# S4 convolution and gated MLP, forward and backward: one PSUM bank for two gradient turns, one product for two planes, other spacing of the lonely transforms

## The chip, the cores and the metric

The kernel runs on one core of a Trainium2 chip, in one launch. The metric is the device time of an execution in microseconds. The chip's engines are called PE (TensorE, matmuls; its weight loads are PEld), DVE (VectorE), ACT (ScalarE), POOL (GpSimd) and SP (SyncE, which here only issues DMAs). Each engine executes its own instructions in the order in which they stand in its queue, and waits there for semaphores of the others.

## What is computed

The forward pass and the gradients (a vjp with `grad_out`) of a layer that adds an S4 convolution and a gated MLP to its input. Shapes: L = 2048 tokens, D = 576 channels, N = 128 states, F = 4608 hidden columns, all bfloat16.

```python
xn = _layernorm(x)
# A: S4. K[d,l] = Re sum_n C[d,n] exp(dt[d] A[d,n] l) dt[d] B[d,n], a causal convolution
Kf = rfft(pad(K)); Uf = rfft(pad(xn.T))
y  = irfft(Uf * Kf)[:, :L].T + xn * Dskip
# B: gated MLP
gate = xn @ W_gate; up = xn @ W_up
gate = gate * (gate > 0)
h = gate * up
out = x + y + h @ W_down
# returned: out, and the gradients for x, A, B, C (re and im), log_dt, Dskip, W_gate, W_up, W_down
```

## The kernel before

Two streams of work are woven into one program. The MLP stream (class `Ffn`, called FFN here) keeps TensorE busy from end to end; the S4 stream (class `S4`) is put between its matmuls.

**FFN.** F is cut into 12 chunks of 384 columns (the loop over `c`), each into 3 blocks `ft` of 128. The tokens are 4 groups `sg` of 4 x 128. For one `(c, sg, ft)`, `a_unit` makes three products of 5 matmuls with 512 columns: gate and up from `xT`, and dh from `gT` (L244). Relu, masks and products on ACT and DVE (L253 to L261) turn them into a tile `T` with three planes: h, and the gradients of gate and up. The planes are needed in two orientations. `outdx` uses them as they are (L298, with the weights `wf`) and gives the outputs `osx`, which POOL's queue adds up in DRAM as `acc_dram` (L311). The weight gradients `dw_down` (L336), `dw_gu` (L352) and `dw_left` (L370) need them turned, in `hN`, `dgN` and `duN`: that is the work of `t_steps` (L270), four transposes of 128x128 into a PSUM tile `ps_mm` and a copy out of it for each plane. The steps of `t_steps` are handed out by `a_unit`, one round after each of its three products, for units that were computed earlier (`turns`), and by `outdx` after its products. `ps_mm` has 5 PSUM banks, the S4 stream's `ps_s4` has 3. Each chunk loads the weights `wd0` to `wd2` through SP's queue (L187) and `wf`, 1296 KB, through ACT's (L191).

**S4.** The channels are two parts `hf` of 288. The convolutions are Fourier transforms in three stages that go through DRAM between them. A forward transform (`fwd1`, L625, then `mix`, L642) makes 16 first steps `n2`, stored as `A_...` (L629), and then 16 mixings `h` that each load a piece of all of these (L706, L774). `product` multiplies spectra on DVE (L664 to L671), `unmix` (L652) and `back2` (L683) go back. `p1` transforms the input and the gradient and brings back `dk`, the gradient of the convolution kernel: `bC1` tiles are loaded (L735) from `C_dk`, which the unmixing stores (L727). `params` computes the coefficient planes `pw` and 36 steps `ex_step` of exponentials: DVE, ACT, and a store of the tile `exs` to `ex_dram` (L585 to L587), with 8 buffers. `p2` generates the convolution kernel and its gradients, 16 channels at a time: DVE makes `xa` (L841), sine and cosine, A, B, X and `XC` (to L866), `turn` makes the kernel's columns (L904), stores them to `k_dram` (L907), transposes and copies `YT`, and `sums` reduces (L928 to L933). `p3` transforms the kernel, loaded as `kk` (L762), and makes the outputs' spectra, stored to `C_ydu` (L793).

`S4.gen` runs: constants; `both(p1(0), params)`; `both(p2(0), p1(1))`; `both(p2(1), p3(0))`; `p3(1)`. `both` weaves a second generator into the first in the ratio of two stated weights. So `p1(0)` and `p3(1)`, with no kernel generation beside them, are the lonely transforms; they have deeper buffers (n = 4 instead of 2).

**What sets the order.** Every generator yields a stated cost in us. The main loop takes FFN's steps one after the other and draws S4's steps as long as S4's stated sum is below `PACE` = 0.9 times FFN's. A larger stated cost in an S4 stage spreads it over more FFN work; `slow(f, task)` multiplies the stated costs of a task by f, and `gap` is a stated cost between stages, in which loads are to land. From the program that is written down in this way, a scheduler orders each engine's queue. `Balance` sends a PSUM copy (L62 on DVE, L68 on ACT) to the engine with the smaller stated sum. The last chunk's `outdx` adds S4's results for each 128 tokens and completes outputs (class `Final`); all of S4 must stand ahead of it.

Memory is reused: the tiles of `p2` (`xa`, `W`) lie where `params` had its buffers.

Of the kernel before, what the change touches and what calls it, by code (L numbers as in the profile page):

```python
# [9 lines left out]
BF16 = mybir.dt.bfloat16  # L10
F32 = mybir.dt.float32
# [12 lines left out]
NK = 5  # L24
# [136 lines left out]
class Ffn:  # L161
    def __init__(self, g, ctx, Wd_in, Wf_in, dWg, dWu, dWd):
        self.g = g
        self.Wd_in, self.Wf_in, self.dWg, self.dWu, self.dWd = Wd_in, Wf_in, dWg, dWu, dWd
        tc, nc = g.tc, g.nc
        pool = lambda name, bufs: ctx.enter_context(tc.tile_pool(name=name, bufs=bufs))
        wp = pool("ffn_w", 1)
        self.wd = [wp.tile([P, NK, Fc], BF16, name=f"wd{i}") for i in range(3)]
        self.wf = wp.tile([P, 3, FTC, D], BF16, name="wf")
        self.hN = wp.tile([P, ST, Fc], BF16, name="hN")  # L170
        self.dgN = wp.tile([P, ST, Fc], BF16, name="dgN")
        self.duN = wp.tile([P, ST, Fc], BF16, name="duN")
# [57 lines left out]
    def a_unit(self, c, sg, ft, turns=()):  # L230

        g, nc = self.g, self.g.nc
        src = self.t_steps(turns)
        xT, gT = self.X[(c, sg)]
        fs = slice(ft * P, (ft + 1) * P)
        pss = []
        dhb = self.dh0.get(ft) if (c, sg) == (0, 0) else None
        for i, rhs in enumerate((xT, xT, gT)):
            if i == 2 and dhb is not None:
                continue  # L240
            w = self.wd[i]
            ps = g.psum_mm.tile([P, 512], F32, name="ps_mm")
            for k in range(NK):
                nc.tensor.matmul(ps[:], lhsT=w[:, k, fs], rhs=rhs[:, k, :], start=(k == 0), stop=(k == NK - 1))  # L244
            pss.append(ps)
            for _ in turns:
                next(src)
            yield NK * 0.2158 + len(turns) * 0.22
        ps_g, ps_u = pss[0:2]
        shp = [P, JS * P]  # L250
        ru = self.ep.tile([P, 2, JS * P], BF16, name="rg")
        upm, rg = ru[:, 0], ru[:, 1]
        nc.scalar.activation(rg, ps_g[:], ACT.Relu)  # L253
        nc.vector.scalar_tensor_tensor(upm, rg, 0.0, ps_u[:], op0=ALU.is_gt, op1=ALU.mult)  # L254
        T = self.tp.tile([P, 3, JS * P], BF16, name="T")
        nc.vector.tensor_tensor(T[:, 0], rg, upm, op=ALU.mult)  # L256
        g.bal.add(d=1.6, a=0.48)
        if dhb is None:
            dhb = self.ep.tile(shp, BF16, name="dhb")[:]
            g.bal.copy(dhb, pss[2][:], 512)  # L260
        nc.vector.tensor_tensor(T[:, 1:3], dhb.unsqueeze(1).to_broadcast([P, 2, JS * P]), ru[:], op=ALU.mult)  # L261
        self.T[(c, sg, ft)] = tuple(T[:, i] for i in range(3))

    def t_steps(self, units):
        g, nc = self.g, self.g.nc
        for c, sg, ft in units:
            for src, dst in zip(self.T[(c, sg, ft)], (self.hN, self.dgN, self.duN)):
                pt = g.psum_mm.tile([P, 512], F32, name="ps_mm")[:].bitcast(BF16).rearrange("p (k t) -> p k t", t=P)
                for j in range(JS):
                    nc.tensor.transpose(out=pt[:, j, :], in_=src[:, j * P:(j + 1) * P], identity=g.ident_bf[:])  # L270
                g.bal.copy(dst[:, sg * JS:(sg + 1) * JS, ft * P:(ft + 1) * P], pt[:, 0:JS, :], 512, fp32=False)
                yield

    def outdx(self, c, sg, j, last=None, turns=()):
# [201 lines left out]
class S4:  # L476
# [85 lines left out]
    def params(self, pw):  # L562
# [3 lines left out]
        with ExitStack() as c:  # L566
            pool = self.pool(c, "par_raw", 1)
            exp_ = self.pool(c, "par_ex", 8)
            raw = pool.tile([P, 6, D], BF16, name="raw")
            nc.sync.dma_start(raw[:], self.par_in[:])  # L570
            ldt = pool.tile([P, D], BF16, name="ldt")
            nc.sync.dma_start(ldt[:], self.log_dt.rearrange("(o d) -> o d", o=1).to_broadcast([P, D]))
            yield 1.0
            dt = pool.tile([P, D], F32, name="dtf")
            nc.scalar.activation(dt[:], ldt[:], ACT.Exp)
            nc.sync.dma_start(self.dt_dram[:], dt[:])
            Ar, Ai, Br, Bi, Cr, Ci = (raw[:, i, :] for i in range(6))
            v.tensor_tensor(pw[:, 0, :], Ar, dt[:], op=ALU.mult)
            bal.add(d=0.7, a=0.7)
            yield 1.0  # L580

            def ex_step(i):
                shp = [P, SX, NE]
                ex = exp_.tile(shp, F32, name="exs")
                v.tensor_tensor(ex[:], pw[:, 0, i * SX:(i + 1) * SX].unsqueeze(2).to_broadcast(shp), self.ev[:].unsqueeze(1).to_broadcast(shp), op=ALU.mult)  # L585
                nc.scalar.activation(ex[:], ex[:], ACT.Exp)
                nc.sync.dma_start(self.ex_dram[:, i], ex[:])  # L587
                bal.add(d=0.75, a=0.65)

            p1 = pool.tile([P, D], F32, name="p1")  # L590
            p2 = pool.tile([P, D], F32, name="p2")
            v.scalar_tensor_tensor(pw[:, 1, :], Ai, 1.0 / TWO_PI, dt[:], op0=ALU.mult, op1=ALU.mult)
            for j, (y1, y2, op) in enumerate(((Br, Bi, ALU.subtract), (Bi, Br, ALU.add))):
                v.tensor_tensor(p1[:], Cr, y1, op=ALU.mult)
                v.tensor_tensor(p2[:], Ci, y2, op=ALU.mult)
                v.tensor_tensor(p1[:], p1[:], p2[:], op=op)
                v.tensor_tensor(pw[:, 2 + j, :], p1[:], dt[:], op=ALU.mult)
                bal.add(d=2.6)
                yield 2.0
            for i in range(D // SX):  # L600
                ex_step(i)
                yield 1.0

# [82 lines left out]
    def p1(self, hf, n, gap):  # L686
# [3 lines left out]
        with ExitStack() as c:  # L690
            ap = self.pool(c, f"p1_a{hf}", n, "right")

            def load(m):
# [1 line left out]
                nc.sync.dma_start(t[:, 0], g.xn_dram[:, 2 * m:2 * m + 2, cols])  # L695
                nc.sync.dma_start(t[:, 1], g.g_v[:, 2 * m:2 * m + 2, cols])
                return lambda i, n2: t[:, i, n2 % 2, :]
            yield from self.slow(1.0 if n < 4 else 1.8, self.fwd1(hf, 2, load, ap, self.pool(c, f"p1_o{hf}", 2 * n - 2 * (n < 4), "right"), n, gap))
        with ExitStack() as c:
            bp = self.pool(c, f"p1_b{hf}", n, "right")  # L700
            fp = self.pool(c, f"p1_f{hf}", n, "right")
# [5 lines left out]
                return b  # L707
            bs = Ahead(load_b, ST, n)
            Z = None
            f = 1.0 if n < 4 else 1.1  # L710
            for h in range(ST + 1):
                old, Z = Z, None
                if h < ST:
# [15 lines left out]
        with ExitStack() as c:  # L729
# [8 lines left out]
            for n2 in range(ST):  # L738
# [7 lines left out]
                g.bal.copy(dk[:, :, n2 % 4, :], self.back2(S3[:, n2 % 2], Ct, 0).rearrange("p (g d) -> p g d", d=SC), DH)  # L746
                if n2 % 4 == 3:
                    nc.sync.dma_start(self.dk_dram[hf][:, n2 // 4], dk[:])
                yield 0.5 if n < 4 else 1

    def p3(self, hf, n, gap):

        g, nc, bal = self.g, self.g.nc, self.g.bal
        with ExitStack() as c:
# [4 lines left out]
            def load(m):  # L759
# [46 lines left out]
    def p2(self, hf, pools, pw):  # L806
# [17 lines left out]
        for gi in range(DH // SC):  # L824
# [7 lines left out]
            for x0 in range(0, SC, SX):  # L832
# [28 lines left out]
                xw = [P, SX, 32]  # L861
                w1 = xp.tile(xs, F32, name="xa")[:].rearrange("p d e -> p (d e)")[:, 0:SX * 32].rearrange("p (d e) -> p d e", e=32)
                w2 = xp.tile([P, 2, SX, NE], F32, name="W")[:].rearrange("p r d e -> p (r d e)")[:, 0:SX * 32].rearrange("p (d e) -> p d e", e=32)
# [72 lines left out]
    def param_grads(self, hf, Sm, pw, xp, yop):  # L936
# [13 lines left out]
        pA, pB, cr, ci = (pw[:, i, hs] for i in range(4))  # L950
# [64 lines left out]
    def gen(self):  # L1015
# [4 lines left out]
        with ExitStack() as cp:  # L1020
# [231 lines left out]
```

## Time and profile before

| What | Value |
|---|---|
| Runs | 1819.53 us median of 3 (1813.02 to 1819.76) |
| Profiled execution | 1819.53 us; span of its instructions 1817.8 us |
| Mean granted clock of PE | 0.987 |
| DMA | 373.30 MB in 239003 packets, mean 205 GB/s |
| Transposes of the turns, L270 on PE | 1728, busy 158.0 us; idle before them 6.2 us |
| Copies of the turns on ACT, 128x512 bf16 | hN 138 x 593 ns, dgN 141 x 600 ns, duN 135 x 606 ns |
| Copies of YT on ACT, 128x1024 bf16 | 1012 ns in most |
| The two coefficient products on DVE, 128x512 f32 | L864 36 x 684 ns, L865 36 x 683 ns |
| wf loads | 11 through ACT's queue, 1296 KB each, median 9.3 us to landing |

A share of busy time is an average over very different stages, so the text below goes by stretches of time, and within a stretch by what an engine waited for. An idle engine costs nothing as long as PE has work; a wait of DVE or ACT counts where a matmul needs the PSUM bank that a copy behind it would free. Matmuls overlap in the pipeline: five with 512 columns in a row start 1.08 us before the work after them, though one is shown with 0.38 us.

### The profile page before, as it was taken

Reading aid. Unit: us, or ns where it says so; the run is one execution under the profiler, and the core shown is the slowest. Engines: PE = TensorE matmul, PEld = TensorE weight load, DVE = VectorE, ACT = ScalarE, POOL = GpSimd, SP = SyncE. Lnnn points to the kernel's source line nnn. Section 1 sums busy time; section 2 is a strip of 40 time slices with the busy share of each in tenths; the row PEclk is TensorE's granted clock in tenths of the full one; section 3 lists DMA queues with packets and bytes.
Section 4 is the critical chain, followed back from the end, with each engine's and each line's share of the span. In section 5 each row is a group of like instructions: output and inputs, shape, how many; then the busy total and the mean of one; then the engine's idle time right before and its main releaser. Section 6 shows DMA issues by size and latency. Waiting matters only on the chain. (4 is left out here: it accounts for less than half of the span.)

```text
span 1817.8 us, 42080 instructions
## 1 busy us (share of the span) xinstructions
PE 1726.3 (95%) x16449; PEld 1188.6 (65%) x16449; DVE 1321.4 (73%) x2875; ACT 1186.7 (65%) x2728; POOL 203.7 (11%) x246
## 2 busy tenths in 40 slices
PE   7979987999999999999999999999999999999998
PEld 5655546667666766767766756666676675576776
DVE  7565875476888878778687789889988864775551
ACT  5865863588488578568558658747756755664651
POOL 0200101021011011111101101201111100110000
PEclk9989988999999999999999999999999999999999
DMA  8789979678667666866856856766675578895873
GB/s 292 266 307 307 325 203 290 183 163 224 195 159 190 206 176 127 245 183 152 232 148 174 238 157 135 195 189 161 148 219 141 102 209 244 240 303 177 262 250 99
DMA packets 239003, 373.30 MB, mean 205 GB/s; under 512 B 49490, under 2 KB 153428, under 8 KB 237268
## 3 DMA queue, kind: packets, MB, share of 16 engines
q1 hardware_dynamic: 212836, 304.09, 51.9%
q0 software_dynamic: 24384, 51.92, 18.6%
q10 hardware_dynamic: 1584, 14.60, 2.2%
q8 instruction: 129, 2.11, 0.5%
q14 instruction: 70, 0.57, 0.1%
HBM read 233.10 MB, written 137.43 MB: 204 GB/s over the span
## 5 line engine op out<-in xcount | busy, mean ns | idle before, releaser
L298 PE MATMUL ps_mm<-wf,T 128*128 128x288 bf16 x3456 | 481.3, 287 | 9.1 <-DVE T L256 5.6
L298 PEld LDWEIGHTS <-T 128*128 128x128 bf16 x3456 | 323.0, 98 | 94.9 <-issue 9.6
L68 ACT CAST osx<-ps_mm 128x288 bf16<-128x288 f32 x684 | 260.8, 426 | 51.7 <-PE ps_mm L298 49.4
L311 POOL DMA_DIRECT2D acc_dram<-osx x160 | 138.2, 864 | 1057.1 <-ACT osx L68 543.2
L352 PEld LDWEIGHTS <-rows 128*128 128x128 bf16 x1536 | 146.3, 98 | 95.9 <-issue 4.6
L244 PE MATMUL ps_mm<-xT,wd_150 128*128 128x512 bf16 x720 | 182.9, 382 | 4.1 <-ACT xT L153 1.6
L270 PEld LDWEIGHTS <-T 128*128 128x128 bf16 x1728 | 128.0, 99 | 87.4 <-issue 7.4
L244 PE MATMUL ps_mm<-xT,wd_151 128*128 128x512 bf16 x720 | 180.2, 380 | 0.0
L244 PE MATMUL ps_mm<-gT,wd_152 128*128 128x512 bf16 x705 | 179.0, 384 | 1.0 <-ACT dgN L68 0.6
L270 PE MATMUL ps_mm<-ident_bf,T 128*128 128x128 bf16 x1728 | 158.0, 221 | 6.2 <-DVE rg L254 1.9
L336 PE MATMUL ps_mm<-rows,hN 128*128 128x144 bf16 x2304 | 158.4, 228 | 0.0
L336 PEld LDWEIGHTS <-hN 128*128 128x128 bf16 x2304 | 150.1, 99 | 3.7 <-issue 1.0
L254 DVE SCALAR_TENSOR_TENSOR rg<-rg,ps_mm 128x512 bf16<-128x512 bf16 x144 | 98.4, 683 | 68.0 <-PE ps_mm L244 41.1
L68 ACT CAST obw<-ps_mm 128x384 bf16<-128x384 f32 x103 | 49.1, 477 | 139.6 <-PE ps_mm L352 98.1
L352 PE MATMUL ps_mm<-dgN,rows 128*128 128x384 bf16 x768 | 137.3, 326 | 0.0
L352 PE MATMUL ps_mm<-duN,rows 128*128 128x384 bf16 x768 | 136.8, 326 | 0.0
L68 ACT CAST dhb<-ps_mm 128x512 bf16<-128x512 f32 x141 | 84.1, 596 | 60.0 <-PE ps_mm L244 58.5
L253 ACT ACTIVATE rg<-ps_mm 128x512 bf16<-128x512 f32 x144 | 87.3, 606 | 49.1 <-PE ps_mm L244 47.0
L261 DVE TENSOR_TENSOR T<-dhb,rg 128x1024 bf16<-128x1024 bf16 x141 | 98.9, 701 | 26.7 <-ACT dhb L68 26.0
L244 PEld LDWEIGHTS <-wd_150 128*128 128x128 bf16 x720 | 67.1, 98 | 65.4 <-issue 7.6
L244 PEld LDWEIGHTS <-wd_152 128*128 128x128 bf16 x705 | 64.0, 98 | 61.0 <-issue 4.4
L244 PEld LDWEIGHTS <-wd_151 128*128 128x128 bf16 x720 | 64.8, 98 | 59.4 <-issue 2.3
(2506 smaller groups left out, 3048.3 us busy)
## 6 DMA issues: line engine op xcount, KB each, us to landing
acc_dram<-osx POOLq DMA_DIRECT2D x176, 288.0 KB, 5.2
gT<-in_gT_dram SPq DMA_DIRECT2D x48, 640.0 KB, 6.1
xT<-xT_dram SPq DMA_DIRECT2D x44, 640.0 KB, 5.7
rows<-in_gq_dram SPq DMA_DIRECT2D x48, 576.0 KB, 4.7
wf<-in_Wf_dram ACTq DMA_DIRECT2D x11, 1296.0 KB, 9.3
ex_dram<-exs SPq DMA_DIRECT2D x36, 320.0 KB, 4.2
ex<-ex_dram SPq DMA_DIRECT2D x36, 320.0 KB, 4.7
out_dram<-obw SPq DMA_DIRECT2D x96, 96.0 KB, 2.7
```

What stands on the lines that cost most here:

```text
L68: self.nc.scalar.copy(out, in_)
L244: nc.tensor.matmul(ps[:], lhsT=w[:, k, fs], rhs=rhs[:, k, :], start=(k == 0), stop=(k == NK - 1))
L253: nc.scalar.activation(rg, ps_g[:], ACT.Relu)
L254: nc.vector.scalar_tensor_tensor(upm, rg, 0.0, ps_u[:], op0=ALU.is_gt, op1=ALU.mult)
L261: nc.vector.tensor_tensor(T[:, 1:3], dhb.unsqueeze(1).to_broadcast([P, 2, JS * P]), ru[:], op=ALU.mult)
L270: nc.tensor.transpose(out=pt[:, j, :], in_=src[:, j * P:(j + 1) * P], identity=g.ident_bf[:])
L298: nc.tensor.matmul(ps[:, cs], lhsT=lt, rhs=rh, start=(i == 0), stop=(i == len(mms) - 1))
L311: nc.gpsimd.dma_start(g.acc_dram[:, t, :, :], o[:], accum_op=ALU.add)
L336: nc.tensor.matmul(ps[:, ft * 144:(ft + 1) * 144], lhsT=self.hN[:, st, ft * P:(ft + 1) * P], rhs=gq[:, st, :], start=(st == 0), stop=(st = ...
L352: nc.tensor.matmul(ps[:, :Fc], lhsT=xs[:, st, 0:P], rhs=src[:, st, :], start=(st == 0), stop=(st == ST - 1))
```

## The change

Three things.

**Turns.** `dgN` and `duN` become two halves of one tile `gN`. `t_steps` now has two steps a unit: the four transposes of h with a copy of 512 columns, then the eight transposes of both gradients into one PSUM tile with one copy of 1024. `a_unit` hands them out in thirds: for one unit in `turns` none after the gate product, one after up, one after dh; for two units 1, 1 and 2. The stated cost of all turns of a unit is the same (0.66).

```diff
-            for _ in turns:
+            n = (2 * len(turns) * (i + 1)) // 3 - (2 * len(turns) * i) // 3
+            for _ in range(n):
                 next(src)
-            yield NK * 0.2158 + len(turns) * 0.22
+            yield NK * 0.2158 + n * 0.33
...
-            for src, dst in zip(self.T[(c, sg, ft)], (self.hN, self.dgN, self.duN)):
+            src, js, fs = self.T[(c, sg, ft)], slice(sg * JS, (sg + 1) * JS), slice(ft * P, (ft + 1) * P)
+            for which in ((0,), (1, 2)):
+                n = len(which) * JS
                 pt = g.psum_mm.tile([P, 512], F32, name="ps_mm")[:].bitcast(BF16).rearrange("p (k t) -> p k t", t=P)
-                for j in range(JS):
-                    nc.tensor.transpose(out=pt[:, j, :], in_=src[:, j * P:(j + 1) * P], identity=g.ident_bf[:])
-                g.bal.copy(dst[:, sg * JS:(sg + 1) * JS, ft * P:(ft + 1) * P], pt[:, 0:JS, :], 512, fp32=False)
+                for i, w in enumerate(which):
+                    for j in range(JS):
+                        nc.tensor.transpose(out=pt[:, i * JS + j, :], in_=src[w][:, j * P:(j + 1) * P], identity=g.ident_bf[:])
+                if n == JS:
+                    g.bal.copy(self.hN[:, js, fs], pt[:, 0:n, :], n * P, fp32=False)
+                else:
+                    g.bal.copy(self.gN[:, :, js, fs], pt[:, 0:n, :].rearrange("p (i j) t -> p i j t", i=2), n * P, fp32=False)
                 yield
```

**Kernel generation.** The two products of the coefficient planes with X become one of twice the size, which reads X's planes twice with an overlap; its result takes the tile W alone and no xa. `pw` keeps its planes 2 and 3 in the other order for it.

```diff
-                v.tensor_tensor(w1, pw[:, 2, hs].unsqueeze(2).to_broadcast(xw), X[:, :, 1:3, :].rearrange("p d r a -> p d (r a)"), op=ALU.mult)
-                v.tensor_tensor(w2, pw[:, 3, hs].unsqueeze(2).to_broadcast(xw), X[:, :, 0:2, :].rearrange("p d r a -> p d (r a)"), op=ALU.mult)
-                v.tensor_tensor(XC[:].rearrange("p d r a -> p d (r a)"), w1, w2, op=ALU.subtract)
+                xv = bass.AP(x.tensor, x.offset, [x.ap[0], (16, 2)] + list(x.ap[1:]))
+                v.tensor_tensor(w, pw[:, 2:4, hs].unsqueeze(3).to_broadcast(xw), xv, op=ALU.mult)
+                v.tensor_tensor(XC[:].rearrange("p d r a -> p d (r a)"), w[:, 1], w[:, 0], op=ALU.subtract)
```

**Spacing.** In the lonely transforms the first steps `fwd1` lose their factors (1.8 in `p1(0)`, 2 in `p3(1)`), the mixing of `p1(0)` goes from 1.1 to 1.25, its way back from 1 to 0.5 a step, the gaps from 6 to 10 and from 6 to 8. The weight of `p1(0)` against `params` goes from 79.04 to 68, and in `params` eight `ex_step` come ahead of the four planes.

```diff
+            for i in range(0, 8):
+                ex_step(i)
+                yield 1.0
...
-            for i in range(D // SX):
+            for i in range(8, D // SX):
...
-            yield from self.slow(1.0 if n < 4 else 1.8, self.fwd1(hf, 2, load, ap, self.pool(c, f"p1_o{hf}", 2 * n - 2 * (n < 4), "right"), n, gap))
+            yield from self.fwd1(hf, 2, load, ap, self.pool(c, f"p1_o{hf}", 2 * n - 2 * (n < 4), "right"), n, gap)
...
-            f = 1.0 if n < 4 else 1.1
+            f = 1.0 if n < 4 else 1.25
...
-                yield 0.5 if n < 4 else 1
+                yield 0.5
...
-            yield from self.slow(1.0 if n < 4 else 2, self.fwd1(hf, 1, load, ap, self.pool(c, f"p3_o{hf}", 2 * n - 2 * (n < 4), "right"), n, gap))
+            yield from self.fwd1(hf, 1, load, ap, self.pool(c, f"p3_o{hf}", 2 * n - 2 * (n < 4), "right"), n, gap)
...
-            yield from self.both(self.p1(0, 4, 6), 79.04, self.params(pw), 45.0)
+            yield from self.both(self.p1(0, 4, 10.0), 68.0, self.params(pw), 45.0)
...
-            yield from self.p3(1, 4, 6)
+            yield from self.p3(1, 4, 8.0)
```

More of the change, by code (lines that the diff above doesn't have):

```diff
@@ L170, in __init__ @@
         self.hN = wp.tile([P, ST, Fc], BF16, name="hN")
-        self.dgN = wp.tile([P, ST, Fc], BF16, name="dgN")
-        self.duN = wp.tile([P, ST, Fc], BF16, name="duN")
+        self.gN = wp.tile([P, 2, ST, Fc], BF16, name="gN")
+        self.dgN, self.duN = self.gN[:, 0], self.gN[:, 1]
         g.xtp = pool("ffn_xt", 2)
@@ L596, in params @@
                 v.tensor_tensor(p1[:], p1[:], p2[:], op=op)
-                v.tensor_tensor(pw[:, 2 + j, :], p1[:], dt[:], op=ALU.mult)
+                v.tensor_tensor(pw[:, 3 - j, :], p1[:], dt[:], op=ALU.mult)
                 bal.add(d=2.6)
                 yield 2.0
-            for i in range(D // SX):
+            for i in range(8, D // SX):
                 ex_step(i)
@@ L860, in p2 @@
                 XC = xop.tile([P, SX, 2, 16], BF16, name="XC")
-                xw = [P, SX, 32]
-                w1 = xp.tile(xs, F32, name="xa")[:].rearrange("p d e -> p (d e)")[:, 0:SX * 32].rearrange("p (d e) -> p d e", e=32)
-                w2 = xp.tile([P, 2, SX, NE], F32, name="W")[:].rearrange("p r d e -> p (r d e)")[:, 0:SX * 32].rearrange("p (d e) -> p d e", e=32)
-                v.tensor_tensor(w1, pw[:, 2, hs].unsqueeze(2).to_broadcast(xw), X[:, :, 1:3, :].rearrange("p d r a -> p d (r a)"), op=ALU.mult)
-                v.tensor_tensor(w2, pw[:, 3, hs].unsqueeze(2).to_broadcast(xw), X[:, :, 0:2, :].rearrange("p d r a -> p d (r a)"), op=ALU.mult)
-                v.tensor_tensor(XC[:].rearrange("p d r a -> p d (r a)"), w1, w2, op=ALU.subtract)
+                xw = [P, 2, SX, 32]
+                w = xp.tile([P, 2, SX, NE], F32, name="W")[:].rearrange("p r d e -> p (r d e)")[:, 0:2 * SX * 32].rearrange("p (w d e) -> p w d e", w=2, e=32)
+                x = X[:, :, 0:2, :].rearrange("p d r a -> p d (r a)")
+                xv = bass.AP(x.tensor, x.offset, [x.ap[0], (16, 2)] + list(x.ap[1:]))
+                v.tensor_tensor(w, pw[:, 2:4, hs].unsqueeze(3).to_broadcast(xw), xv, op=ALU.mult)
+                v.tensor_tensor(XC[:].rearrange("p d r a -> p d (r a)"), w[:, 1], w[:, 0], op=ALU.subtract)
                 bal.add(d=6.5, a=2.5)
@@ L949, in param_grads @@
         S_r, S_i, T_r, T_i = Sm[:, 0, :, 0], Sm[:, 1, :, 0], Sm[:, 0, :, 1], Sm[:, 1, :, 1]
-        pA, pB, cr, ci = (pw[:, i, hs] for i in range(4))
+        pA, pB, ci, cr = (pw[:, i, hs] for i in range(4))
         ob = lambda: yop.tile([P, DG, 2, P], BF16, name="Y")[:].rearrange("p d r q -> p (d r q)")[:, 0:DH]
```

## The prediction

> **What bounds the kernel now.** First the page's busy shares and its span in stretches (time; then per engine busy us and instructions; granted TensorE clock; DMA share; GB/s).
>
> ```profile
> PE 1726.3 (95%) x16449; PEld 1188.6 (65%) x16449; DVE 1321.4 (73%) x2875; ACT 1186.7 (65%) x2728; POOL 203.7 (11%) x246
> ```
> ```profile
> 90.90:136.30 45.40, 35.06 (x300) 27.02 (x299) 29.79 (x53) 29.08 (x65) 3.41 (x7) 0.85 0.88 307
> ...
> 227.20:272.70 45.50, 37.81 (x261) 21.87 (x259) 32.01 (x81) 31.17 (x78) 4.23 (x5) 0.89 0.72 203
> 272.70:318.10 45.40, 34.52 (x344) 27.40 (x345) 23.23 (x52) 17.85 (x40) 6.66 (x7) 0.89 0.97 290
> ...
> 499.90:545.30 45.40, 44.79 (x439) 29.94 (x436) 37.77 (x76) 38.06 (x88) 7.88 (x8) 1.00 0.68 159
> ...
> 1499.70:1545.10 45.40, 41.85 (x305) 25.71 (x304) 21.52 (x50) 22.80 (x56) 3.45 (x4) 1.00 0.83 243
> ```
>
> TensorE sets the end: 1726.3 of 1817.8 us busy, so 91.5 us are waits. A typical stretch (499.9) loses 0.6 us. Three early ones lose 10.3, 7.7 and 10.9 us, and 15%, 11% and 11% of their busy time to a lower clock (5.3, 4.2, 3.8 us): 42 us together. Those are the lonely transforms of part 0, and the change reshapes exactly them. TensorE's waits, longest first:
>
> ```profile
> PE ps_s_4349 L683 <- DMA wf<-in_Wf_dram: 6.1, 1, 6.1
> PE ps_s_1939 L625 <- DVE fA_1905 L62: 5.7, 1, 5.7
> PE ps_mm L298 <- DVE T L256: 5.6, 6, 2.0
> PE ps_s_4032 L683 <- DMA bC_3933<-C_dk_183: 4.6, 1, 4.6
> PE ps_s_3633 L642 <- DVE s_ug L62: 4.6, 1, 4.6
> PE ps_s_25313 L625 <- DMA kk<-k_dram_190: 3.2, 1, 3.2
> PE ps_s_25381 L625 <- DMA kk<-k_dram_190: 3.2, 1, 3.2
> ...
> PE ps_s_3645 L642 <- DVE s_ug L62: 2.0, 1, 2.0
> ```
>
> Two of them only pass on a DVE that stands at a DMA. VectorE's timeline in both places:
>
> ```profile
> 129.37 0.82 DVE L585 TENSOR_TENSOR exs<-pw,ev 128x640 f32<-128x640 f32 x1 [5.51 <-DMA ex_dram<-exs]
> 130.12 0.45 DVE L62 CAST fA_1905<-ps_s_1931 128x288 bf16<-128x288 f32 x1
> ```
> ```profile
> 242.60 0.82 DVE L841 TENSOR_TENSOR xa<-pw,ev 128x640 f32<-128x640 f32 x1 [9.36 <-DMA ex_dram<-exs]
> ```
>
> The first waits for one of the 8 exs buffers, whose store was issued together with the wf load of ScalarE's queue; the second is the first xa of kernel generation, whose memory the last exs tiles still occupy. Behind both stand the copies that free PSUM for the transforms. The wf load also stretches other transfers (DMA issues of 262 to 306 us: KB, us to landing):
>
> ```profile
> wf<-in_Wf_dram ACTq DMA_DIRECT2D x1, 1296.0 KB, 10.3
> ...
> bC_3933<-C_dk_183 SPq DMA_DIRECT2D x1, 144.0 KB, 4.5
> ...
> bC_4265<-C_dk_183 SPq DMA_DIRECT2D x1, 144.0 KB, 13.0
> ```
>
> **The change part by part.** Distances below are PE time: the matmuls between two places in the built order, each at its issue interval in TensorE's timeline (0.216 us for 512 columns, 0.162 for 384, 0.122 for 288, 0.063 for 144, 0.056 for a transpose). In this measure the order becomes: first DFT of part 0 from 78.5-125.7 to 78.5-109.2; its mixing 137.6-204.4 to 128.5-203.2; its DFT back 215.9-235.7 to 216.6-230.7; kernel generation's first turn 254.5 to 246.9; first DFT of the last p3 1389.7-1407.6 to 1379.4-1391.7; its last unmix 1506.6 to 1490.4; the final loop's first matmul stays at 1517.3.
>
> (1) *The wait of xa, -8.7 us.* Before, the last exs store stood in SP's queue behind 20 transfers of the mixing and left at 234.5; xa came right after. In the new order eight ex steps come first and the rest run at a higher ratio, so that the last store leaves at PE time 169.8 (188.6 before), and xa stands on VectorE behind two more products and the five dskip operations: some 12 us of its work (by the rows' 0.3 to 0.7 us each) after that store, where these stores need 4 to 9 us to land. The wait should be gone: 4.6 + 2.0 us, and half of the stretch's 4.2 us of clock. Bounds: 0 (it still waits in full) to -10.8.
>
> (2) *The DFT back beside wf, -8.0 us.* The last bC load is issued at PE time 228.4 and wf at 233.3 (before: 230.1 and 231.8, with the load landing after 13.0 us). Gone: 6.1 us and half of 3.8 us of clock. Bounds 0 to -9.9.
>
> (3) *Its first load, -2.0 us.* The gap of 10 instead of 6 puts 9.5 us of matmuls, not 7.5, between the last unmix and the first bC matmul; the 4.6 us wait shrinks by that. Bounds -4.6 to 0.
>
> (4) *The DFT back at half the stated cost, +5 us.* With five bC buffers each load can go out only after the use five steps earlier; that was some 5 us of matmuls ahead of its own use and is now 3.7 to 6.3, from which SP takes 0.5 us an issue and a wait for the dk copy ahead of two loads. Landing took 3.7 to 7.0 us without wf. About four loads are late by 1 to 1.5 us. Bounds 0 and 11 (four chained waits of 7.0 - 4.2 us).
>
> (5) *First DFT of part 0, -4.4 us.* The exs buffers no longer meet wf (eight stores leave before it): -5.7 and half of 5.3 us of clock. Against it, sig loads 7 and 8 go out with wf (landing some 10 us, their matmuls 7 to 8 us later): +2.6. VectorE was busy from 97.1 to 121.4 but for 1.1 us, and by the rows' durations its queue between PE times 80 and 100 holds 29.9 us instead of 28.6 (some eight of the transform's copies come earlier): +1.3. Bounds -9 and +4.
>
> (6) *First DFT of the last p3, +3 us.* The kk loads are still 5.1 and 5.5 us of matmuls ahead of their use (5.6 and 5.4), so 6.4 us of waits stay. The 32 copies of 0.43 us fall into 12 us instead of 18, nearly all on ScalarE, whose queue holds 15.5 us of work for PE time 1380-1390 (12.4 in the worst ten before), partly inside the kk waits. Between its last matmul and the first mixing there are 5.5 us where 7.1 just sufficed: +1.6. Bounds -3 and +8. That S4 then ends 16 us earlier gives nothing: it was done 10.7 us ahead of the final loop already.
>
> (7) *Turns, -5 us.* Transposes stay 1728. Of 432 copies 144 go. ScalarE's pairs took 600 + 606 ns; a 128x1024 bf16 copy out of PSUM is there as YT's, 1012 ns: 194 ns each, 135 times, 26 us off an engine that is 65% busy. On the path counts only what TensorE waits for: 6.2 us before L270 (T not ready, or no free bank), of which half goes, as the first turn of a unit now comes after the up product and gate and up gradients last; and a bank less per turn (five banks, six tiles a unit before, five now), 2 us. The 1012 ns copy can hold a Relu or a transform's copy 0.4 us longer: bounds -10 and +2.
>
> [...]
>
> (8) *Generation, -0.5 us.* Two 128x512 f32 products (684 + 683) become one of 1024. From 512 and 640 columns (683, 820) the slope is 1.07 ns, so 1231 ns (bounds 683 and 1366): 36 x 135 = 4.9 us off VectorE. Its cover is TensorE's queue; TensorE waits for V L932 in several 0.4 to 2.3 us pieces, of which this takes little (0 to -2).
>
> (9) *Everything from 250 on stands 6 to 8 us earlier against the FFN, +3 us.* The waits of the middle (about 1 us a stretch) fall anew; since I removed the visible ones above, I charge for one new wait of the 3.2 us kind. Bounds -5 and +8.
>
> Sum: -8.7 - 8.0 - 2.0 + 5 - 4.4 + 3 - 5 - 0.5 + 3 = -17.6 us. The profiled execution took 1819.53 us (span 1817.8), which is also the median of the three: 1801.9, **1802 us**.
>
> The clock matters for (4). After the 5.74 us wait before 130.62 the next 23 matmuls of 144 columns took 2.76 us to the next start, not 1.45, and after a wait of 2.28 us at 105.37 six of 288 columns took 1.4 instead of 0.7 us. So by the rows even short waits can cost up to 1.3 us more, and (4) could be +8.
>
> [...]
>
> **Rivals.** *Waits only move.* For it: TensorE is at 95%, ScalarE and VectorE are not its limit, every removed wait stands ahead of another load (bC behind C_dk, kk behind k_dram). Against: xa's is a plain ordering accident. If (1), (2) and (5) give half, 10.5 us, and (4) and (6) cost 12 with (7) at -2, the sum is about +3 with (9): 1819 +- 9.
>
> *Slower: packed transforms run at landing time.* If loads land in 6.5 to 7 us as they did at 284-290 beside the wd loads, the eleven later bC loads go five per 7.5 us, 16 us for 14 us of matmuls, and every short wait halves the clock: (4) +14. The last p3 does the same with kk at 7.8 us and ScalarE's 5.5 us of excess: (6) +10. With only (1) and half of (2) gained (-12.7) and nothing in (5) and (7), +14.3 with (9): about 1834. It decides from a landing over 6 us in the DFT back; for it speaks the DMA share of 0.97 there, against it the 3.7 to 4.6 us of most loads before 283.
>
> *The merged copy does nothing* ((7) = 0): 1807, still in the forecast's case.
>
> **Chances and range.** Forecast 0.58, waits only move 0.26, slower 0.16. What a measurement of this kernel tells from no change is about 0.5%, 9 us. Faster (under 1810.4) is the forecast, plus 0.03 of the second case less 0.01 of its own tail: 0.60; same 0.25; slower 0.15. The forecast alone reaches 1788 to 1812 with its terms' bounds not all on one side; taking in the second case and the near end of the third, 1788 to 1824.
>
> **What would show it.** (1): the first xa of generation without a DMA wait over 2 us, stretch 227-273 over 42 us busy at clock near 1. (2)-(4): no wait over 4 us at the DFT back, several of 1 to 2. (5): no DMA wait of exs over 3 us. (6): two kk waits near 3 us each, and s_k's first matmul late by 1 to 2. (7): ScalarE's busy time 15 to 30 us lower. Wrong if the three early stretches still lose over 35 us, or the DFT back or the last p3 over 12 each.

## The result, and the profile after

| | Before | After |
|---|---|---|
| Runs on one chip | 1818.69 us median of 4 (1813.02 to 1819.76) | 1798.58 us median of 4 (1795.32 to 1799.02) |
| Ratio | | 0.9892, 95% interval 0.9868 to 0.9916 |
| Profiled execution, its span | 1819.53, 1817.8 us | 1798.99, 1797.1 us |
| Mean granted clock of PE | 0.987 | 0.994 |

The change makes the kernel 1.1% faster, 20 us. A second measurement on another chip gave 0.9898 (below). The forecast was 1802 us, and faster.

The busy shares of the page after, then its span in the same stretches as shown for the kernel before (time; busy us and instructions of PE, PEld, DVE, ACT, POOL; granted clock; DMA share; GB/s):

```profile
PE 1719.4 (96%) x16449; PEld 1183.1 (66%) x16449; DVE 1313.0 (73%) x2821; ACT 1176.0 (65%) x2602; POOL 204.2 (11%) x246
```
```profile
90.90:136.30 45.40, 38.91 (x351) 29.14 (x349) 32.24 (x59) 33.37 (x81) 3.44 (x7) 0.92 0.91 319
136.30:181.80 45.50, 42.74 (x281) 25.05 (x282) 26.01 (x54) 23.81 (x51) 0.00 (x0) 0.92 0.91 296
227.20:272.70 45.50, 37.86 (x278) 22.42 (x276) 37.00 (x91) 30.04 (x72) 5.08 (x6) 1.00 0.85 227
272.70:318.10 45.40, 41.30 (x430) 31.53 (x427) 20.32 (x44) 19.86 (x45) 8.39 (x8) 1.00 0.95 285
1499.70:1545.10 45.40, 38.53 (x287) 24.42 (x286) 23.40 (x64) 31.72 (x81) 4.31 (x5) 0.96 0.96 279
```

Idle time and lost clock together (span less busy, and busy times one less clock): the first stretch loses 6.5 + 3.1 us where it lost 10.3 + 5.3; that of 227 loses 7.6 and no clock (7.7 + 4.2 before), that of 273 4.1 and no clock (10.9 + 3.8). The stretch of 136 and that of 1500 got worse: 2.8 + 3.4 where the kernel before lost 1.5 and no clock, and 6.9 + 1.5 (3.6 and no clock). TensorE's waits, longest first (L635 is now the first transform, L652 mix, L662 unmix, L693 back2, L305 outdx):

```profile
PE ps_mm L211 <- DMA gT<-in_gT_dram: 8.6, 1, 8.6
PE ps_s_2130 L635 <- DVE fA_2098 L62: 5.7, 1, 5.7
PE ps_s_25047 L652 <- DMA b_k<-A_k_177: 4.6, 1, 4.6
...
PE ps_s_3583 L662 <- DVE s_ug L62: 2.3, 1, 2.3
PE ps_s_4057 L693 <- DMA bC_4009<-C_dk_182: 2.3, 1, 2.3
...
PE ps_s_3993 L693 <- DMA bC_3864<-C_dk_182: 1.4, 1, 1.4
...
PE ps_s_24810 L635 <- DMA kk<-k_dram_189: 1.1, 1, 1.1
```

The first of them is the start of the program: the kernel before waits 9.1 us there, which its list ahead leaves out. Gone are the 6.1 us at wf, the 4.6 us of the first bC load (now 1.4), the 4.6 us behind xa (2.3 us are left), and the two kk waits of 3.2 us (1.1). Two waits are new: 5.7 us in the first transform of part 0 again, in another place, and 4.6 us at the first load of p3's mixing.

The first of these, in VectorE's timeline, in SyncE's queue (start, us, line, out<-in), and in that queue's own waits from 95 to 182 us:

```profile
137.82 0.82 DVE L592 TENSOR_TENSOR exs<-pw,ev 128x640 f32<-128x640 f32 x1 [6.54 <-DMA ex_dram<-exs]
```
```profile
122.15 0.74 SPq L706 DMA_DIRECT2D sig<-in_grad_out_dram  x1
129.57 0.33 SPq L330 DMA_DIRECT2D rows<-xs_dram_141  x1
...
131.43 1.07 SPq L594 DMA_DIRECT2D ex_dram<-exs  x1
```
```profile
SPq L330 <- DMA wf<-in_Wf_dram: 6.6, 1, 6.6
```

SyncE issued nothing from 122.9 to 129.6, where it stood at a rows load, and it stood there for wf. The rows load and the wf load share no data. But in the trace both count on the same semaphore (109), and the rows load waits until the transfer before it on that semaphore has landed: wf, issued at 120.44 through ScalarE's queue and landed at 129.50. The ninth ex store, ready since some 115 us but behind the rows load in the queue, left at 131.43 and landed at 137.79, and VectorE waited 6.54 us for the buffer that this store frees. Copies of fA stand behind that instruction, and TensorE behind the copies. The second measurement shows the same: 5.1 us of SyncE's queue at wf, 5.14 us of VectorE at exs.

### The profile page after: what moved, and what is told of

It reads as the page before. It is cut to its first block, busy times and chain, and to the rows that moved or that the text cites. A ratio compares the mean times of both kernels' runs of the same rounds, so it can differ in the third digit from the quotient of the medians.

```text
span 1797.1 us, 41897 instructions
## 1 busy us (share of the span) xinstructions
PE 1719.4 (96%) x16449; PEld 1183.1 (66%) x16449; DVE 1313.0 (73%) x2821; ACT 1176.0 (65%) x2602; POOL 204.2 (11%) x246
## 3 DMA queue, kind: packets, MB, share of 16 engines
q0 software_dynamic: 24384, 51.92, 18.9%
## 5 line engine op out<-in xcount | busy, mean ns | idle before, releaser
L305 PE MATMUL ps_mm<-wf,T 128*128 128x288 bf16 x3456 | 480.6, 287 | 10.9 <-DVE rg L255 3.2
L305 PEld LDWEIGHTS <-T 128*128 128x128 bf16 x3456 | 324.5, 98 | 100.3 <-issue 16.7
L68 ACT CAST osx<-ps_mm 128x288 bf16<-128x288 f32 x681 | 256.0, 435 | 47.4 <-PE ps_mm L305 45.7
L359 PE MATMUL ps_mm<-gN,rows 128*128 128x384 bf16 x1536 | 265.2, 326 | 0.0
L274 PEld LDWEIGHTS <-T 128*128 128x128 bf16 x1728 | 119.5, 98 | 58.5 <-DVE T L262 0.7
L343 PEld LDWEIGHTS <-hN 128*128 128x128 bf16 x2304 | 149.4, 99 | 10.3 <-issue 8.0
L68 ACT COPY gN<-ps_mm 128x1024 bf16<-128x1024 bf16 x136 | 140.1, 1030 | 8.8 <-PE ps_mm L274 8.5
L274 PE MATMUL ps_mm<-ident_bf,T 128*128 128x128 bf16 x1728 | 141.1, 220 | 0.3 <-DVE T L262 0.2
L262 DVE TENSOR_TENSOR T<-dhb,rg 128x1024 bf16<-128x1024 bf16 x141 | 100.7, 714 | 25.3 <-ACT dhb L68 24.6
L244 PEld LDWEIGHTS <-wd_150 128*128 128x128 bf16 x720 | 66.2, 98 | 63.2 <-issue 6.1
```

Source lines behind the costliest of these rows:

```text
L68: self.nc.scalar.copy(out, in_)
L274: nc.tensor.transpose(out=pt[:, i * JS + j, :], in_=src[w][:, j * P:(j + 1) * P], identity=g.ident_bf[:])
L305: nc.tensor.matmul(ps[:, cs], lhsT=lt, rhs=rh, start=(i == 0), stop=(i == len(mms) - 1))
L343: nc.tensor.matmul(ps[:, ft * 144:(ft + 1) * 144], lhsT=self.hN[:, st, ft * P:(ft + 1) * P], rhs=gq[:, st, :], start=(st == 0), stop=(st = ...
L359: nc.tensor.matmul(ps[:, :Fc], lhsT=xs[:, st, 0:P], rhs=src[:, st, :], start=(st == 0), stop=(st == ST - 1))
```

## The experiments

All ratios are to the kernel before, on the same chip and in the same rounds. To see where time is lost, one number is read from each trace: the time at a place less TensorE's work up to it (the matmuls in the built order, each at the issue interval that the prediction used). It takes out that S4's work stands elsewhere. The places are the first matmul of `dw_left` of chunks 0, 1 and 9 (at 179.6, 351.9 and 1515.0 us in the kernel before), and the end. So the first column holds the first DFT of part 0, the second the rest of p1(0) and the begin of generation, the third the middle, the last p3(1) and what follows.

| Kernel | Median us | Ratio, 95% interval | to 180 | to 350 | to 1515 | to the end | Loss in all |
|---|---|---|---|---|---|---|---|
| before (profiled 1819.53) | | | 36.6 | 35.8 | 65.9 | 23.6 | 161.9 |
| after (profiled 1798.99) | 1798.58 | 0.9892, 0.9868 to 0.9916 | 35.7 | 22.2 | 60.0 | 23.3 | 141.2 |
| after, again | 1796.74 | 0.9898, 0.9883 to 0.9913 | 34.4 | 21.8 | 59.5 | 23.4 | 139.1 |
| 1 turns alone | 1815.19 | 1.0008, 0.9992 to 1.0023 | 38.8 | 25.3 | 66.7 | 23.8 | 154.7 |
| 2 spacing alone | 1794.39 | 0.9888, 0.9869 to 0.9908 | 34.6 | 22.1 | 57.6 | 22.5 | 136.8 |
| 3 generation alone | 1814.62 | 1.0000, 0.9987 to 1.0013 | 37.1 | 29.4 | 63.2 | 21.7 | 151.4 |
| 4 last p3 alone | 1814.44 | 1.0001, 0.9985 to 1.0017 | 37.9 | 33.3 | 65.3 | 22.5 | 159.1 |
| 5 ex order alone | 1806.46 | 0.9945, 0.9928 to 0.9962 | 32.4 | 22.9 | 65.3 | 22.9 | 143.5 |
| 6 p1 spacing alone | 1798.73 | 0.9914, 0.9896 to 0.9932 | 40.5 | 20.4 | 57.7 | 21.8 | 140.4 |
| 7 after, ex stores on GpSimd | 1808.24 | 0.9960, 0.9944 to 0.9975 | 50.6 | 19.1 | 58.8 | 22.4 | 150.9 |
| 8 after, generation 6 us later | 1807.54 | 0.9963, 0.9949 to 0.9978 | 35.1 | 24.8 | 66.3 | 23.8 | 149.9 |
| 9 before, generation 6.5 us earlier | 1807.78 | 0.9956, 0.9943 to 0.9968 | 36.6 | 33.2 | 59.5 | 22.9 | 152.2 |
| 10 recombined | 1804.50 | 0.9939, 0.9927 to 0.9951 | 34.9 | 23.6 | 67.9 | 18.9 | 145.2 |
| 11 after, generation 4 us earlier | 1808.33 | 0.9956, 0.9943 to 0.9968 | 34.0 | 25.2 | 72.0 | 16.5 | 147.8 |

The losses are those of one execution. How far they scatter is seen where kernels share an order. Kernel 4 is the kernel before up to its last p3: 37.9, 33.3 and 65.3 us against 36.6, 35.8 and 65.9; the changed kernel's two profiles differ by 1.3, 0.4 and 0.5. Kernels 1, 3 and 9 too keep the old order of p1(0) and params, and lose 25.3 to 33.2 us in the second column; in the first, these five kernels with the old order lose 36.6 to 38.8. The kernel before is itself uneven: its runs beside these kernels took 1807.6 to 1821.6 us, those of the changed kernel 1795.3 to 1799.0.

### The three parts, each alone

Kernel 1 is the kernel before with `t_steps`, `a_unit` and `gN` of the change.

> The kernel before with the new turns alone. Theory A (the gain is the spacing of the lonely transforms, the turns give the forecast's term (7)): 5 us less than before, 1814, ratio 0.997; ScalarE's busy time about 11 us lower as in the changed kernel, and the three early stretches keep their waits of 6 us (wf, xa, exs). Rival B (the gain is ScalarE's freed time and the bank): 15 us less or more, 1804, ratio 0.992.

Kernel 2 has all spacing edits and nothing else.

> The kernel before with the new spacing alone (both lonely transforms, the eight early ex steps, the weight); turns and generation as before. Theory A: 12 to 15 us less, 1804 to 1807, ratio 0.992 to 0.9935; the xa wait and the 6.1 us wf wait are gone. Rival B: the waits only move, 1819 within 4 us, ratio 0.998 to 1.002.

Kernel 3 has the merged product with the swapped planes 2 and 3 of `pw`.

> The kernel before with the merged coefficient product alone. Theory A: 0 to 2 us less, ratio 0.999 to 1.000, as VectorE's 5 us lie behind TensorE's queue. Rival B: the DVE queue is the bound of generation and the whole 5 us show, ratio 0.997.

Kernel 4 has the two edits of the last p3.

```diff
-            yield from self.slow(1.0 if n < 4 else 2, self.fwd1(hf, 1, load, ap, ...))
+            yield from self.fwd1(hf, 1, load, ap, ...)
...
-            yield from self.p3(1, 4, 6)
+            yield from self.p3(1, 4, 8.0)
```

> The kernel before with the change of the last p3 alone (no factor of 2 on its first steps, gap 8 for 6). Theory A: 1 to 4 us slower, ratio 1.000 to 1.002: the kk waits shrink from 6.4 to about 1, but the first mixing waits some 4 us for its load b_k and S4 was done ahead of the final loop in any case. Rival B: faster by 3 to 5 us, since the two kk waits of 3.2 us go, ratio 0.998.

The turns gave nothing that can be told from zero, less than either theory expected; its profiled execution, at 1812.4 us below its own median, is a favourable one. Spacing alone is as fast as the whole change, and better than theory A expected. Generation and the last p3 gave nothing; rival B falls for both. In kernel 4 the waits are not those that theory A named: 3.5 us at kk and 0.4 at the first mixing, for 1 and 4. So the gain is the spacing of p1(0) and params, all of it; part of it works through the place that it gives to generation (below).

Why the turns are worth so little is seen in ScalarE's timeline. In the kernel before:

```profile
716.79 0.63 ACT L68 COPY dgN<-ps_mm 128x512 bf16<-128x512 bf16 x1
717.26 0.65 ACT L68 CAST dhb<-ps_mm 128x512 bf16<-128x512 f32 x1
717.73 0.66 ACT L68 COPY duN<-ps_mm 128x512 bf16<-128x512 bf16 x1
```

A copy of 512 columns is shown with 0.63 us, but the next one starts 0.47 us after it: copies in a row overlap. So two of them hold ScalarE for less than the 1.2 us of the sum, and one copy of 1024 columns (1024 ns) takes the place of less. The page's busy time, which counts overlapped time once, went from 1186.7 to 1175.9 us in kernel 1. That is 10.8 us for 137 merged copies on ScalarE, 79 ns each, and not the 194 ns that the durations gave. Balance is not the cause: in kernel 1 ScalarE has 684 copies of osx with 288 columns, as before.

### Which spacing: the ex order, or the pace of p1(0)

Kernel 5 has the ex order and the weight alone:

```diff
+            for i in range(0, 8):
+                ex_step(i)
+                yield 1.0
...
-            for i in range(D // SX):
+            for i in range(8, D // SX):
...
-            yield from self.both(self.p1(0, 4, 6), 79.04, self.params(pw), 45.0)
+            yield from self.both(self.p1(0, 4, 6), 68.0, self.params(pw), 45.0)
```

> The kernel before with eight ex steps first and the weight 68 alone; p1's spacing, turns, generation and the last p3 as before. Theory A (the stops of VectorE at the ex stores are half of the gain): terms (1) and (5), 8 to 12 us less, ratio 0.9935 to 0.9955; no DMA wait of xa over 2 us. Rival B (the stop moves to another store or another load): within 3 us, ratio 0.998 to 1.002.

Kernel 6 has the pace of p1(0) alone: no factor 1.8, 1.25 for the mixing, 0.5 for the way back, gap 10.

> The kernel before with the spacing of p1(0) alone (no factor 1.8, mixing 1.25, way back 0.5, gap 10); ex steps, weight, turns, generation and the last p3 as before. Theory A (the way back clear of wf is the other half): terms (2) to (4), 5 us less, with another 5 where generation stands 7 us earlier: 8 to 12 us less, ratio 0.9935 to 0.9955; the 6.1 us wf wait gone, xa's wait still there. Rival B (the ex order is all of it): within 3 us.

They take 10 us and 16 us less. For kernel 5 theory A holds. For kernel 6 rival B falls, and the gain is larger than A's 8 to 12: its generation stands 7.6 us of TensorE's work earlier, as in the changed kernel, and the middle alone is 8.2 us better, while kernel 5 has generation at the old place. The two don't add up to the 20 us of kernel 2, because they share the second column: 22.9 with the one, 20.4 with the other, 22.1 with both. VectorE has no DMA wait at xa in kernel 5 (8.5 us in kernel 4, which stands for the kernel before there); TensorE's waits from 174 to 345 us, in kernel 4, 5 and 6:

```profile
PE ps_s L683 <- DMA bC<-C_dk: 9.4, 3, 3.9
PE ps_s L642 <- DVE s_ug L62: 6.7, 2, 3.7
```
```profile
PE ps_s L686 <- DMA bC<-C_dk: 7.7, 3, 3.9
...
PE ps_s L645 <- DVE s_ug L62: 0.4, 1, 0.4
```
```profile
PE ps_s L642 <- DVE s_ug L62: 4.3, 1, 4.3
PE ps_s L683 <- DMA bC<-C_dk: 4.2, 2, 4.0
```

The ex order takes the wait behind xa (6.7 to 0.4 us), the pace takes half of that at the way back (9.4 to 4.2).

In the first column they seem to work against each other, though by little more than the scatter: kernels with the old order lose 36.6 to 38.8 us, the ex order alone 32.4 (34.9 in kernel 10, which has the same first DFT), the denser first DFT alone 40.5, and both together 34.4 to 35.7. In the middle kernel 5 gains nothing (65.3).

### The stop at the ex stores

Kernel 7 asks whether SyncE's standing queue causes the 6.54 us wait shown above.

```diff
-                nc.sync.dma_start(self.ex_dram[:, i], ex[:])
+                nc.gpsimd.dma_start(self.ex_dram[:, i], ex[:])
```

> The changed kernel with the ex stores on GpSimd's queue in place of SyncE's. Theory A (the 5.7 us stop in the first DFT of part 0 comes from SyncE's queue, which stood 6.7 us at a rows load, and not from wf's traffic): the exs wait of 6.5 us and TensorE's 5.7 us wait go, 4 to 7 us less than the changed kernel, ratio to before 0.9855 to 0.987. Rival B (wf's transfer delays the store whatever the queue): within 1.5 us of the changed kernel, ratio 0.988 to 0.990, exs still waits over 4 us.

Neither came true: the stop is gone, as A has it (2.70 us is the longest wait of an exs), and the kernel is 10 to 12 us slower than the changed one. The stretch from 136 us in kernel 7, and the mixing's loads in it, in the changed kernel and then in kernel 7 (KB, median us to landing):

```profile
136.30:181.80 45.50, 31.96 (x226) 19.58 (x225) 22.04 (x35) 24.25 (x44) 12.95 (x24) 0.83 0.92 348
```
```profile
b_ug<-A_ug_178 SPq DMA_DIRECT2D x8, 288.0 KB, 4.7
```
```profile
b_ug<-A_ug SPq DMA_DIRECT2D x5, 288.0 KB, 11.3
```

The stretch moves 348 GB/s instead of 296, and TensorE is busy for 32.0 us of it instead of 42.7. Without the other transfers of SyncE's queue ahead of them, the stores ran freely: 21 of 320 KB were issued from 140.8 to 167.1 us. SyncE's own transfers then crawled, and it stood itself (first line, the waits of its queue in this stretch; the second is ScalarE's timeline):

```profile
SPq L364 <- ACT obw L68: 8.1, 1, 8.1
```
```profile
175.49 0.48 ACT L68 CAST obw<-ps_mm 128x384 bf16<-128x384 f32 x1 [8.71 <-DMA out_dram<-obw]
```

An obw store of 96 KB, issued at 163.02, took 12.4 us to land (the median of the changed kernel is 2.7). A copy on ScalarE waited 8.71 us for the buffer that it frees, TensorE 8.8 us for the PSUM bank that the copy frees, and SyncE 8.1 us for the copy, whose result it was to store next. So the stop of VectorE does come from SyncE's order, as A said, but A was wrong to leave out wf: the queue stood for wf's landing, as shown above. Kernel 7 takes the stores out of that queue altogether, so the run does not tell the order of the queue from the shared semaphore; a rows load that need not wait for wf was not tried. The old order was also what held the stores back. That the DMA engines are the scarce thing here fits these rows, but was not tested by itself.

### The shift of the middle

Kernel 8 puts generation back where it stood before the change, kernel 9 puts it forward in the kernel before, kernel 11 further forward in the changed kernel.

```diff
             yield from self.both(self.p1(0, 4, 10.0), 68.0, self.params(pw), 45.0)
+            yield 6.0
```

Kernel 9 has `yield -6.5` after its own such line, kernel 11 `yield -4.0`.

> The changed kernel with a stated cost of 6 us between p1(0) and generation, so that generation stands against the FFN exactly where it stood before (first turn at 254.5 us of TensorE's work, not 246.9). Theory A (term (9) had the wrong sign: the middle gained 5 to 8 us from the shift alone): it is 4 to 8 us slower than the changed kernel, ratio to before 0.9915 to 0.9935, with the loss between 350 and 1515 us. Rival B (the shift is worth nothing): within 2 us of the changed kernel, ratio 0.988 to 0.990.

> The kernel before with a stated cost of -6.5 us between p1(0) and generation: generation stands against the FFN where the changed kernel has it (first turn at 246.9 us of TensorE's work, not 254.5), and nothing else differs. Theory A (the shift alone is worth 6 to 8 us in the middle): TensorE's loss between 352 and 1466 us falls from 64 to about 57 us; ahead of that the xa wait grows by up to 5 us; in sum 2 to 8 us less, ratio 0.9955 to 0.999. Rival B (the middle gains only with the new p1 spacing): no change in the middle, ratio 1.000 to 1.003.

> The changed kernel with a stated cost of -4 us between p1(0) and generation: first turn at 242.7 us of TensorE's work instead of 246.9. Theory A (the shift has no direction: the middle's waits fall anew): the waits of the middle change by 3 to 8 us either way, and xa comes too early for its store, 1 to 4 us; ratio to before 0.986 to 0.994, likelier slower than the changed kernel. Rival B (earlier is better in itself): 3 to 5 us faster than the changed kernel.

Theory A has the direction of all three and the size of kernel 9; kernels 8 and 11 are slower than it said. The middle goes from 60 to 66.3 us in kernel 8 and from 65.9 to 59.5 in kernel 9: the shift alone makes the kernel before 0.44% faster. Further forward (kernel 11) it is 72.0, the worst of all, though the last stretch gains 7 us.

The whole table says the same. In six rows the first matmul of `sums` stands at 251.2 us of TensorE's work (after, its repetition, kernels 2, 6, 7 and 9): their middles lose 57.6 to 60.0 us. In six it stands at 257.7 (before, kernels 1, 3, 4, 5 and 8): 63.2 to 66.7. Whatever else differs between them, the place of generation sorts the middle.

So a large part of the 20 us is the shift. It is worth 8 us in the kernel before, and the changed kernel without it (kernel 8) is only 0.37% faster than the kernel before, 7 us (4 to 9 by the interval). Where the middle's loss sits in kernel 8 is seen in TensorE's waits from 340 to 1495 us, in the second run of the changed kernel and then in kernel 8:

```profile
PE ps_s L924 <- DVE V L942: 5.8, 9, 1.8
```
```profile
PE ps_s L924 <- DVE V L942: 12.0, 15, 2.0
```

The turn of YT (L924) waits for a PSUM bank that `sums` holds until VectorE has made its products from it (V, L942). Generation has the same instructions in both, but meets other units of the FFN on VectorE's queue: 15 waits instead of 9. This does not explain every row. Kernel 9 waits 6.2 us there, kernels 4 and 5 with generation at the old place 6.4, and still kernel 9's middle is 6 us better: its gain is spread over other waits, and why they fall so is not shown.

### A version from the useful parts

Kernel 10 keeps what seemed to pay: the ex order (its edit is as in kernel 5) and weight, the way back at 0.5, and the same place of generation; the first DFT keeps its factor, the mixing 1.1, the gap 6, and turns, generation and p3 are as before.

```diff
-                yield 0.5 if n < 4 else 1
+                yield 0.5
...
-            yield from self.both(self.p1(0, 4, 6), 79.04, self.params(pw), 45.0)
+            yield from self.both(self.p1(0, 4, 6), 68.0, self.params(pw), 45.0)
+            yield 1.0
```

> The kernel before with the ex order and weight of the change and the way back of p1(0) at 0.5, and 1 us of stated cost before generation so that it stands at 246.9 us as in the changed kernel; the first steps keep their factor 1.8, mixing 1.1, gap 6; turns, generation and the last p3 as before. Theory A (the gain is the ex order, the way back clear of wf and the shift; the packed first DFT, turns, generation and the last p3 add nothing): as fast as the changed kernel or up to 8 us faster, ratio to before 0.985 to 0.989. Rival B (the packed first steps or the turns are needed): 5 us or more slower than the changed kernel, ratio 0.992 or more.

> The changed kernel once more, beside the others of this call: 0.9892 is expected, within 0.002.

It is 8 us slower than the changed kernel, as rival B's number has it, but not for its reason: the first two columns are as good as the changed kernel's, and all of the loss is in the middle (67.9 against 59.5). Its first turn stands at 246.9 us of TensorE's work as in the changed kernel, its first sums at 249.9 instead of 251.2 (kernel 11, with 72.0, has them at 246.4). That this is what let the waits fall otherwise fits, but is not shown. No version was found that beats the changed kernel by more than the intervals; spacing alone equals it.

## Why the prediction was right, and where it was not

The time (1802 against 1798.6 us) and the likeliest case were right, and the mechanism in part: the waits named in (1) to (3) went. But 8 us of the gain or more came with the shift (9), which was charged as a loss. Kernel 8 has all of the change but the shift: it gained 7 us, where the terms without (9) forecast 20.6. By stretches, the forecast had -4.4, -13.7, -2.5 (the turns, generation and the shift) and +3 us; the two profiled executions show -0.9, -13.6, -5.9 and -0.3.

- **(1) to (4), the rest of p1(0): -13.7 forecast, -13.6 measured.** The xa wait, the wf wait and most of the first bC wait (4.6 to 1.4) went as said, and the way back pays with waits of 0.5 to 2.3 us at bC, 5.1 us in sum for the +5 of (4). A single execution flatters the term: the five kernels with the old order of p1(0) and params lost 25.3 to 35.8 us there, 31.4 on average, which would make the usual gain some 9 us. Nor are (1) and (2) to (4) a sum, as kernels 5 and 6 show: each has most of the gain alone.
- **The clock, as weighed in (4).** The rows of the kernel before allowed +8 for (4); that the sum has +5 was the author's estimate, and no row of them shows it. In the changed kernel the waits of the way back, of 0.5 to 2.3 us, left the clock alone: it was 1.00 from 216.5 to 300 us. But the length of a wait does not decide it: TensorE waited 2.37 us up to 104.13 and 2.29 us up to 275.71, and only the first was followed by half the clock. In the clock's records of the two traces, of the kernel before and of the changed kernel, every stretch of half the clock but the last, which the end of the records cuts, lasts 3.41 us or a multiple of it (3.41, 6.83 or 10.24), and each begins a multiple of 3.41 us after the first record: in these traces the clock changes on a grid of 3.41 us. The windows of this grid around the two waits, each with one behind it (PE's busy time first, granted clock third from the end):

```profile
100.43:103.84 3.41, 1.33 (x13) 0.87 (x12) 3.41 (x6) 3.41 (x7) 0.00 (x0) 1.00 1.02 398
104.00:108.00 4.00, 3.10 (x10) 1.08 (x10) 4.00 (x9) 3.81 (x12) 0.00 (x0) 0.50 0.94 327
```
```profile
271.09:274.50 3.41, 2.33 (x19) 1.33 (x18) 2.94 (x7) 1.29 (x3) 0.00 (x0) 1.00 1.05 342
274.50:277.91 3.41, 2.20 (x25) 1.91 (x26) 3.41 (x12) 1.65 (x4) 0.00 (x0) 1.00 0.95 291
275.60:279.60 4.00, 3.89 (x38) 3.07 (x39) 3.92 (x10) 3.31 (x8) 0.00 (x0) 1.00 0.97 360
```

The first wait fell into one window, which was idle for 2.1 of its 3.41 us; the second was split over two, which kept 2.3 and 2.2 us of work. Counted over the full-clock windows of the grid in both traces: of those in which TensorE was idle for more than 60% of the time, 8 of 8 were followed by half the clock; of those idle for 45 to 60%, 4 of 9; of the 1013 others, none. So by these traces a wait of some 2 us may cost the clock or not, and for these two it went with where they fell on the grid.
- **(5), first DFT of part 0: -4.4 forecast, -0.9 measured (-2.2 in the second execution).** This step failed. "The exs buffers no longer meet wf (eight stores leave before it)" is not so: the ninth store stood in SyncE's queue behind a rows load, and that load stood 6.6 us for wf's landing. The ex order was worth 4.2 us in kernel 5 and 1.7 in kernel 10, not 8.3. The costs set against it, 3.9 us, were 3.9 in kernel 6, or 1.7 against the least favourable of the kernels with the old order.
- **(6), last p3: +3 forecast, -0.3 measured** (kernel 4: 1.0001). The kk waits did not stay: 1.1 us are left of 6.4. The first mixing was late by 4.6 us, not 1.6. The two errors cancelled. Of the +3 only 1.6 us are worked out under it; the rest, it seems for ScalarE's longer queue, is not.
- **(7), turns: -5 forecast, nothing measured** (1.0008; in the middle 0.8 us more than before, and 2 us more in the changed kernel than in kernel 2). The 26 us, from durations that overlap, were 10.8. The half of the idle time ahead of the transposes that was to go did go, as the line shows (busy us, mean ns, idle before):

```profile
L274 PE MATMUL ps_mm<-ident_bf,T 128*128 128x128 bf16 x1728 | 141.1, 220 | 0.3 <-DVE T L262 0.2
```

Against kernel 2, which has the same spacing, 4.7 us went there (5.0 to 0.3) and 3.2 came back at outdx, whose largest group of matmuls waits 10.9 us where it waited 7.7, most of it for rg and T. Those are made by VectorE, which the turns don't relieve. In kernel 1 the transposes' idle time falls as well (6.2 to 1.1) and outdx has only 0.6 us more; where the rest went in its usual execution is not shown. "The merged copy does nothing" was the case for this term.
- **(8), generation: -0.5 forecast, 0.0 measured** (1.0000). The merged product takes 1217 ns where 1231 were worked out.
- **(9), the shift: +3 forecast, a gain of 8 us and more measured** (8 us in kernel 9; kernel 8, without it, is 9 to 13 us slower than the changed kernel; 6 us of either lie in the middle). The sign was wrong, and the bounds, -5 to +8, did not hold it. The forecast took it that a well spaced middle can only lose by a shift; the table shows that it had lost 66 us all along, and that nearby places give between 57.6 and 72.0.

Of the rivals, "waits only move" described two terms correctly, (5) and (6), where a wait went and another came. "Packed transforms run at landing time" did not decide: TensorE's waits at bC came to 6.5 us in sum, its loads landed in 3.6 to 7.5 us, and the clock stayed at 1.00 in that stretch. That the total fell within 4 us is in good part luck: (9) was off by 11 us or more one way, and (1) to (5) and (7) together by about as much the other.

## What to carry to other kernels

Read the cost of a short instruction from the starts of two in a row, not from the duration that is shown: for copies out of PSUM on ScalarE that made 0.47 of 0.63 us, and a merge that seemed to save 26 us saved 11 on an engine that did not bound. When an engine waits for a store, ask what the store's queue stood for: here it was a load of another queue, by way of a semaphore. Giving the stores another queue removed this wait and made a longer one, so ask too what else the standing queue was holding back. And where two streams are woven by stated costs, an edit that shortens an early stage shifts the whole rest: test the shift alone, with a bare cost between the stages, before putting the gain down to the edit.

## What had not been expected of the hardware

- Copies out of PSUM on ScalarE overlap (0.63 us shown, 0.47 us from start to start); one of 1024 columns in place of two of 512 took 79 ns off the busy time.
- With GpSimd's stores beside them (348 GB/s over 45 us), SyncE's transfers landed late: an obw store of 96 KB took 12.4 us, where the median of the changed kernel is 2.7.
- A rows load in SyncE's queue stood 6.6 us for a wf load in ScalarE's, with which it shares no data but a semaphore.
- Of two waits of TensorE of 2.3 and 2.4 us one was followed by half the clock for 6.8 us, the other by the full clock. On the traces' grid of 3.41 us, only the first left TensorE idle for more than 60% of a window.
